# Decode in two stretches around the 256-column phase, P of three steps kept on chip, and a step's load put back

## The chip, the core and the metric

The kernel runs on one core of a Trainium2 chip. The metric is the device time of one execution in microseconds: the median over several runs. A profiled execution is used to read where the time goes; its times are counted in us from the first instruction (the span).

## The reference

Four batches of eight heads run a gated delta rule over 768 tokens with head size 48; the result goes through a mixture of four dense experts and then through a gated feed-forward block:

```python
for t in range(S):                              # attention, state is 48 x 48 per head
    y[:, :, t] = einsum('bhd,bhde->bhe', q[:, :, t], state)
    v_old = einsum('bhde,bhd->bhe', state, k_n[:, :, t])
    state = state + beta_t * outer(k_n[:, :, t], v[:, :, t] - v_old)
x = y as (3072 tokens, 384)
for e in range(4):                              # w1: 384 x 1024, w2: 1024 x 384
    out += p[:, e] * (relu(x @ w1[e]) @ w2[e])  # p: domain_probs, normalized
result = (sigmoid(out @ w_gate) * (out @ w_val)) @ w_out   # 384 x 1536 and back
```

All inputs are float32. The kernel gets the feed-forward block's weights as 64-bit words (`wp2`).

## The kernel before

**Products.** Every float32 product of the MoE is made of three matmuls in a rounded format: the weights are split into a high part (ScalarE, line 223) and a rest (VectorE, line 224), the tokens likewise. Weights come in granules of 128x768 floats (384 KB): `w_load` asks for one on SP's queue into one of three raw buffers, `w_split` splits it into one of four split buffers, `granule` does both some granules ahead of their use.

**Phases.** The 768 tokens of each sequence are cut into 12 steps of 64; a step has 256 columns of tokens, a pair of steps 512. A pair goes through the four experts ("m1") and then through the block ("m2"). Only the first pair is cut differently: expert 0 runs over step 0 alone, expert 1 over both steps, then comes expert 0 over step 1 alone, and so on. These two phases with 256 columns use up a granule in half the time. `EVENTS` lists the matmul groups of all phases in order.

**Attention steps.** Step c needs the matrices L and P (products of keys with keys and with queries, masked), the inverse X of a triangular matrix made from L (`inv_ops` on VectorE, two steps in one run, moved through DRAM to `XT` and `Ld`), and then a chain of small matmuls (`chain`): `ks_task`, `half_task` twice for the first runs, `tb_task`, `y_task`, `s_task`. The start-up makes L and P of steps 2 and 3 in the tiles `LP[0]` and `LP[1]`, masks them there, and those of steps 4 and 5 in DRAM (`raw_d`), from where `plan_g` fetches them into the same two tiles: step c uses `LP[c % 2]`, `Lts` and `Pts` are its two halves. `p_out` stores P of a step in DRAM (`pd`), `load_ys` reads it back into `YQ`, in two halves of 64 partitions, when the step's turn comes.

**Decode.** The 36 blocks ("parts") of the feed-forward block's weights arrive as 64-bit floats and are turned into 32-bit ones on the way: `dec_load` asks SP for 384 KB into one of five buffers, `dec_scale` is two operations on ScalarE (lines 264 and 265), `dec_join` three on VectorE, and `dec_store` puts 192 KB into `w2_d` from GpSimd's queue. The result of a part stands in one of four buffers up to part 7, in one of nine from part 8. All parts share memory with the inverse's tiles and later token tiles.

**Order.** Nothing is scheduled by the hardware: each engine runs its own list in order, and the lists are written by a planner at build time. `now` is the planned time, which grows by the matmuls of the MoE alone (a 512-column unit of an expert takes 3.885, a 256-column one 1.965; the phase over step 1 alone is planned from about 43 to 61). `plan(t, fn)` puts work at a planned time; `slot` emits what is due between matmul groups, `fill` emits the decode and the inverse from two lists, each in order. `pe_at` counts the matmuls emitted, attention included; `vec_at` is the planner's estimate of VectorE. Work marked "dve" is held while `vec_at` is more than `SLACK` = 2.8 ahead of `pe_at`. An emitted instruction still waits for its data; SP in particular issues each DMA only when its buffer is free, and what stands behind it on SP waits too.

Of the kernel before, what the change touches and what calls it, by code (L numbers as in the profile page):

```python
# [33 lines left out]
READ = 16.0  # L34
SERIAL = 0.12
FLIP, MOVE = 2, 4.0
INV2 = 0.0, 0.5, 78.0
AHEADD, LD, LS = 1.5, 6.0, 6.0
WARM = 11
WARM0, WARM1 = 2, 16  # L40
DEC0, DEC1, MORE = 17.0, 162.0, 8
CH1, CH2, TR1, TR2 = 66.0, 42.0, 42.0, 14.0

INV = [((0, 1), True), ((2, 3), True)]
# [25 lines left out]
NG1, NG2 = len(ORDER1) // 2, len(ORDER2) // 2  # L70
# [44 lines left out]
def moe_delta_kernel(  # L115
# [14 lines left out]
    nc = tc.nc  # L130


    pe_at, vec_at = [0.0], [0.0]
# [124 lines left out]
    def dec_load(n):  # L258
        dec_at[n] = pe_at[0]
        nc.sync.dma_start(out=dec_views(n)[0].bitcast(I32), in_=wp2[n].bitcast(I32))  # L260

    def dec_scale(n):
        r, low, high, t = dec_views(n)
        nc.scalar.activation(out=t, in_=high.bitcast(F32), func=AF.Copy, scale=2.0**-112)
        nc.scalar.activation(out=low, in_=low.bitcast(U32), func=AF.Copy, scale=2.0**-29)

    def dec_join(n):
        r, low, high, t = dec_views(n)
        ti = t.bitcast(I32)
        ts, stt, tt = vec.tensor_scalar, vec.scalar_tensor_tensor, vec.tensor_tensor  # L270
        return [
            lambda: ts(out=high, in0=high, scalar1=-(2**31), scalar2=None, op0=ALU.bitwise_and),
            lambda: stt(out=ti, in0=ti, scalar=3, in1=high, op0=ALU.logical_shift_left, op1=ALU.bitwise_or),
            lambda: tt(out=ti, in0=ti, in1=low, op=ALU.add),
        ]

    def dec_store(n):
        stored[0] = n + 1
        dec_at[n] = pe_at[0]
        nc.gpsimd.dma_start(out=w2_d[n // 2, :, (n % 2) * DM : (n % 2 + 1) * DM], in_=dec_views(n)[3])  # L280

    def plan_decode(t0, t1):
        def later(n, wait):
            return n < 0 or pe_at[0] > dec_at[n] + wait

        total = 2 * NG2
        gap = (t1 - t0) / total
        items = []
        for n in range(total):
            t = t0 + gap * n  # L290
            items.append((t - AHEADD * gap, "", lambda n=n: dec_load(n), lambda n=n: later(n - 5, LS)))
            items.append((t, "", lambda n=n: dec_scale(n), lambda n=n: later(n, LD)))
            for j, fn in enumerate(dec_join(n)):
                items.append((t + gap * (0.3 + 0.15 * j), "dve", fn))
            items.append((t + gap * 2.0, "", lambda n=n: dec_store(n)))
        items.sort(key=lambda r: r[0])
        back["dec"] += items


    x_hi, x_lo = {}, {}  # L300
# [20 lines left out]
    def load_ys(c):  # L321
        load_ki(c)
        if c == 1:
            return
        (q[1] or q[0]).dma_start(out=YQ[64:112, 0], in_=kq[c, 64:112, 1])
        (q[1] or q[0]).dma_start(out=YQ[0:C, 1], in_=kq[c, 0:C, 1])
        pd = pd_t.pop(c).rearrange("p (i h t) -> p i h t", i=2, h=H)
        q[0].dma_start(out=YQ[0:C, 0], in_=pd[0:C])
        q[0].dma_start(out=YQ[C:P, 1], in_=pd[C:P])
# [406 lines left out]
    def norm_late(c, i):  # L736
        t = tp.tile([P, 2 * STEP], F32, tag="tmp", name="kn2")[:, :DM]
        nc.sync.dma_start(out=t, in_=kt[c, :, i * DM : (i + 1) * DM])

        def rest():  # L740
            nc.scalar.square(out=t, in_=t)
            vec.tensor_reduce(
                out=w_all[:, 2 * c + i], in_=t.rearrange("p (h d) -> p h d", d=D), op=ALU.add, axis=mybir.AxisListType.X
            )

        return rest

    def plan_norms(c, t):
        for n in range(2):
            box = []  # L750
            plan(t + 13.0 * n, lambda c=c + n, box=box: box.extend(norm_late(c, i) for i in range(2)))
            plan(t + 13.0 * n + 7.0, lambda box=box: [fn() for fn in box])
        plan(t + 21.0, lambda: norms(c, c + 2))
        plan(t + 35.0, lambda: norm_move(c, c + 2))

    def norms(c0, c1):
        sl = slice(2 * c0, 2 * c1)
# [17 lines left out]
    def norm_move(c0, c1):  # L775
        sl = slice(2 * c0, 2 * c1)
        to, at = (t[:, sl].rearrange("p (c i) h -> p c i h", i=2) for t in (nrm_v, nrm_all))
        for i in range(2):
            for b in range(2):
                (q[1] or q[0]).dma_start(out=to[HALVES[i], :, b], in_=at[HALVES[b], :, i])  # L780
# [161 lines left out]
    def plan(t, fn, kind=""):  # L942
        todo.append((t, len(todo), kind, fn))
# [61 lines left out]
    def plan_chain(c, t, gap):  # L1005
        rows = chain(c)
        if c > 1:
            plan(t - (9.0 if c < 4 else 7.0 if c % 2 else 16.0), lambda: scale_v(c))
        if c > 1 and c % 2 == 0:

            def first():
                while inv_done[0] <= INV_OF[c][0]:
                    back["inv"].pop(0)[2]()
                if c > 2:
                    x_in(c)

            def one(n):
                q[2] = nc.sync
                put(*(x_parts(c) + off_parts(c))[n])

            plan(t - (30.0 if c == 2 else 13.0), first)
            for n in range(6 if c == 2 else 0):
                plan(t - 23.0 + 2.6 * n, lambda n=n: one(n))
        for r, row in enumerate(rows):
            plan(t + gap * r, lambda row=row: [fn() for fn in row], "pe")
        t1 = t + gap * len(rows)
        if c % 2 == 0 and c:
            plan(t1 - 2 * gap, lambda: (x_in(c + 1), off_in(c + 1)))
        if c >= FLIP:
            for n, fn in enumerate(x_move(c)):  # L1030
                plan(t1 - (2 if c < NC - 1 else 1) * gap + 4.0 + 1.4 * n, fn)
        if c + 1 < NC:
            plan(t + 2 * gap, lambda: (load_v(c + 1), load_ks(c + 1)))
            plan(t1 + 3.0 if c > 1 else 75.0, lambda: load_ys(c + 1))
        return t1
# [8 lines left out]
    def leave(c):  # L1044
        q[0] = nc.sync if c < 6 else nc.gpsimd
        l_out(c)
        p_out(c)
        q[0] = nc.gpsimd

    def plan_g(c, t):  # L1050
# [190 lines left out]
    with tc.manual_schedule():  # L1241
        pre_lo = xp.tile([P, KT, 2 * STEP], F32R, tag="xlo", name="pre_lo")
        dec_tiles()
        dpt = startup()
        q[1] = nc.sync
        vec_at[0] = 0.0
        plan(0.0, lambda: (gate_probs(dpt), load_p(0), load_p(1)))
        for i in range(2):
            plan(0.0, lambda i=i: s_task(0, i), "pe")
        plan(0.0, lambda: load_ys(1))  # L1250
        for c in (2, 3):
            back["dec"].append((4.0 + c, "dve", lambda c=c: (scale_p(c), p_out(c))))
        plan_chain(1, 1.0, 1.9)
        plan_tr(1, 12.0, 1.0)
        plan_inv(1, *INV2)
        plan_decode(DEC0, DEC1)
        for k in range(1, NPAIR):
            w = W[k]
            if k > 1:
                r0 = max(M2[0] + 44.0, w - 262.0)  # L1260
                plan_inv(k, r0, r0 + 17.0, w - CH1 - 20.0)
            if k + 1 < NPAIR:
                g0 = w - (161.0 if k > 1 else 116.0)
                plan_norms(2 * k + 2, g0 - 12.0)
                plan_g(2 * k + 2, g0)
                plan_g(2 * k + 3, g0 + 26.0)
            plan_chain(2 * k, w - (CH1 if k > 1 else 87.0), 5.9)
            plan_chain(2 * k + 1, w - (CH2 if k > 1 else 50.0), 5.9)
            plan_tr(2 * k, w - (TR1 if k > 1 else 26.0), 4.0)
            plan_tr(2 * k + 1, w - (TR2 if k > 1 else 9.0), 4.0)  # L1270
        todo.sort(key=lambda r: (r[0], r[1]))

        T, h = 0.0, {}
        for what, n, us in EVENTS:
            kind, b, e, s0, ns = PHASES[n]
            part = unit_us(kind, ns) / (2 if kind == "m1" else 3)
            if what == "b":
                now[0] = T = T + part * len(us)
                emit_b(n, us, [h.pop((n, u)) for u in us])
                slot()  # L1280
                continue
            if kind == "m1" and us[0] == 0:
                need = [(2 * b + s0 + s, i) for s in range(ns) for i in range(2)]
                while not all(q in x_done for q in need):
                    todo.pop(0)[3]()
            now[0] = T = T + part * (1 if kind == "m1" else 2)
            h[n, us[0]] = emit_a(n, us[0])
            slot()
            if us[0] == 3 and 0 < n < len(PHASES) - 1:
                load_p(n + 1)  # L1290
# [72 lines left out]
```

## Time and profile before

| | us |
|---|---|
| median of three runs | 1435.51 (1432.78 to 1441.81) |
| the profiled execution | 1437.48 |
| its span, first to last instruction | 1435.6 |
| TensorE busy (matmuls) | 1387.8 |
| VectorE busy | 1023.8 |
| ScalarE busy | 559.2 |

A windows row gives, for each stretch, its length and the busy time of PE, PEld, DVE, ACT and POOL in this order, with the count of instructions in brackets, then the granted clock of TensorE as a share of full speed, the busy share of the 16 DMA engines and what they moved. PE is TensorE's matmuls, PEld its weight loads, DVE VectorE, ACT ScalarE, POOL GpSimd, SP the engine that issues most DMAs. Tiles are shown without their numbers, so YQ stands for YQ and YQ1, and the buffers of the decode have the names of the tiles whose memory they use (dec_a, dec_b, Lpp).

### The profile page before, as it was taken

To read this page: it belongs to the slowest core of one execution; us is meant where nothing else is said; L and a number is where in the kernel's file an instruction comes from. 1 tells how busy PE (TensorE), PEld (TensorE's weight loads), DVE (VectorE), ACT (ScalarE), POOL (GpSimd) and SP (SyncE) were. 2 spreads that over 40 slices of the span, in tenths; PEclk is the share of its full clock that TensorE was granted. 3 is DMA by queue.
4 is the path that set the end of the run, shared out by engine and by line. 5 is a ranking of instruction groups with operands and counts; after the bars stand their busy time and mean duration, and the time that the engine had idled before them with its cause. 6 is when DMAs were issued, how large, how long until landed. Compare 5 with 4: busy or idle time off the path is not lost.

```text
span 1435.6 us, 25201 instructions
## 1 busy us (share of the span) xinstructions
PE 1387.8 (97%) x9939; PEld 1143.9 (80%) x9939; DVE 1023.8 (71%) x1809; ACT 559.2 (39%) x919; POOL 170.6 (12%) x235
## 2 busy tenths in 40 slices
PE   6889898999999999999999999999999999999998
PEld 5778776788878788888888788888888888888887
DVE  7658786866999677888667788767777755444553
ACT  3335453644323344332344432344333344333343
POOL 2310220310012210011300001310000210000000
PEclk6789999999999999999999999999999999999999
DMA  8876796995455874555765555775434662434331
GB/s 210 243 207 213 229 312 239 283 248 153 154 163 143 184 194 143 165 158 154 190 159 165 161 163 144 178 194 153 138 97 128 151 185 94 136 107 128 96 106 65
DMA packets 114790, 241.52 MB, mean 168 GB/s; under 512 B 38784, under 2 KB 43072, under 8 KB 113008
## 3 DMA queue, kind: packets, MB, share of 16 engines
q1 hardware_dynamic: 94368, 191.72, 44.2%
q0 software_dynamic: 15904, 46.23, 13.8%
q10 hardware_dynamic: 4400, 1.97, 0.6%
q8 instruction: 78, 1.28, 0.4%
q14 instruction: 40, 0.33, 0.1%
HBM read 197.38 MB, written 29.02 MB: 158 GB/s over the span
## 4 chain that ended last, share of the span: by engine, by line
PE 81%; DVE 7%; DMA 5%; issue 3%; SPq 1%; ACT 1%; POOL 1%; ACTq 0%; DVEq 0%; POOLq 0%
PE ph L834 43%; PE acc L871 33%; DVE Xpp L142 2%; DVE itmp L142 2%; DVE ws L142 1%; DMA raw<-in_wp 1%; PE pu L597 1%; DVE hlo L142 1%; PE ps L683 1%; PE pk L597 1%; PE pg L362 1%; PE yt L639 1%; DMA XT<-xd 1%; DMA dec_a<-in_wp 1%; PE yt L640 1%
## 5 line engine op out<-in xcount | busy, mean ns | idle before, releaser
L834 PE MATMUL ph<-xhi,ws 128*128 128x512 f32 (+1 forms) x2064 | 629.2, 388 | 8.2 <-DVE ws L142 6.9
L871 PE MATMUL acc<-hhi,ws 128*128 128x512 f32 (+1 forms) x1632 | 496.7, 386 | 8.1 <-DVE ctmp L142 3.0
L834 PEld LDWEIGHTS ph<-xhi,ws 128*128 128x128 f32 x2064 | 381.4, 188 | 87.1 <-DVE ws L142 7.7
L834 PE MATMUL ph<-xlo,ws 128*128 128x512 f32 (+1 forms) x1032 | 395.5, 386 | 0.6 <-DVE xlo L142 0.6
L871 PEld LDWEIGHTS acc<-hhi,ws 128*128 128x128 f32 x1632 | 304.0, 189 | 72.3 <-issue 6.0
L142 DVE TENSOR_TENSOR ws<-raw,ws 128x768 fp32r<-128x768 f32 x308 | 294.3, 961 | 40.0 <-ACT ws L223 36.7
L871 PE MATMUL acc<-hlo,ws 128*128 128x512 f32 (+1 forms) x816 | 314.3, 385 | 3.8 <-issue 1.9
L841 ACT ACTIVATE hhi<-ph 128x512 fp32r<-128x512 f32 (+1 forms) x200 | 116.2, 581 | 472.1 <-PE ph L834 465.1
L223 ACT CAST ws<-raw 128x768 fp32r<-128x768 f32 x308 | 251.9, 829 | 18.8 <-DMA raw<-in_wp 12.0
L142 DVE SCALAR_TENSOR_TENSOR hlo<-ph,hhi 128x512 fp32r<-128x512 f32 (+1 forms) x200 | 133.4, 667 | 148.1 <-ACT hhi L841 147.7
L834 PEld LDWEIGHTS ph<-xlo,ws 128*128 128x128 f32 x1032 | 194.2, 189 | 41.3 <-DVE xlo L142 2.5
L871 PEld LDWEIGHTS acc<-hlo,ws 128*128 128x128 f32 x816 | 154.3, 189 | 35.7 <-DVE hlo L142 3.2
L142 DVE TENSOR_TENSOR itmp<-Xpp,Lpp 128x62 f32<-128x62 f32 (+29 forms) x344 | 157.6, 465 | 6.5 <-DMA Lpp<-ls 1.1
L142 DVE TENSOR_TENSOR Xpp<-Xpp,itmp 128x62 f32<-128x62 f32 (+29 forms) x344 | 157.2, 464 | 5.8
L142 DVE TENSOR_TENSOR gv<-ph,sg 128x512 f32<-128x512 f32 x72 | 49.7, 691 | 95.6 <-PE ph L834 92.0
L850 ACT CAST hhi<-gv 128x512 fp32r<-128x512 f32 x72 | 44.7, 621 | 165.4 <-DVE gv L142 165.4
L142 DVE TENSOR_TENSOR hlo<-gv,hhi 128x512 fp32r<-128x512 f32 x72 | 50.2, 697 | 49.4 <-ACT hhi L850 49.4
L913 POOL DMA_DIRECT2D ACC<-ctmp x39 | 34.5, 1174 | 390.8 <-DVE ctmp L142 390.8
L848 ACT ACTIVATE sg<-ph 128x512 f32<-128x512 f32 x72 | 43.0, 597 | 42.8 <-PE ph L834 42.8
L442 POOL DMA_DIRECT2D ld<-LP x12 | 8.1, 675 | 322.9 <-DVE LP L142 231.5
L142 DVE TENSOR_TENSOR ctmp<-acc,pe 128x512 f32<-128x512 f32 (+1 forms) x57 | 35.4, 657 | 9.8 <-PE acc L871 9.1
L582 POOL TENSOR_TENSOR V<-V,nrm_v 128x384 f32<-128x384 f32 x22 | 22.1, 1044 | 37.8 <-DMA V<-in_vt 24.7
(171 smaller groups left out, 854.9 us busy)
## 6 DMA issues: line engine op xcount, KB each, us to landing
raw<-in_wp SPq DMA_DIRECT2D x200, 384.0 KB, 3.1
raw<-w_d SPq DMA_DIRECT2D x108, 384.0 KB, 3.5
ACC<-ctmp POOLq DMA_DIRECT2D x33, 256.0 KB, 5.6
KQ<-in_kg SPq DMA_DIRECT2D x7, 896.0 KB, 6.7
Lpp<-ld POOLq DMA_DIRECT2D x8, 768.0 KB, 9.1
pe<-p_d SPq DMA_DIRECT2D x23, 256.0 KB, 5.3
dec_a<-in_wp SPq DMA_DIRECT2D x15, 384.0 KB, 6.6
Lpp<-in_wp SPq DMA_DIRECT2D x14, 384.0 KB, 7.2
```

The costliest lines, as they stand in the source:

```text
L142: return fn(*args, **kw)
L223: nc.scalar.copy(out=w[:, 0], in_=t)
L362: nc.tensor.matmul(out=pg[i][b * C : (b + 1) * C, j], lhsT=src[b][ROWS[i], 0, h], rhs=src[b][ROWS[i], :, h], start=True, stop=True,)
L582: nc.gpsimd.tensor_tensor(out=V[:, b], in0=V[:, b], in1=nrm_v[:, 2 * c + b].unsqueeze(2).to_broadcast([P, H, D]), op=ALU.mult,)
L597: nc.tensor.matmul(out=ps[r][HALVES[k], h], lhsT=lhsT, rhs=rhs, start=True, stop=True)
L639: nc.tensor.matmul(out=dst[:, 0], lhsT=fa[:, cols], rhs=YQ[0:112, 0, i, h], start=True, stop=True)
L834: nc.tensor.matmul(out=res[q], lhsT=lt, rhs=rt, start=(k == 0 and j == 0), stop=(k == KT - 1 and j == 2))
L841: nc.scalar.activation(out=hh, in_=res[0], func=AF.Relu)
L848: nc.scalar.activation(out=sg, in_=res[0], func=AF.Sigmoid)
L850: nc.scalar.copy(out=hh, in_=gv)
L871: nc.tensor.matmul(out=acc_t[d][:, :w], lhsT=lt, rhs=rt, start=(u == 0 and j == 0), stop=(u == nf - 1 and j == 2),)
L913: nc.gpsimd.dma_start(out=a, in_=t, accum_op=ALU.add)
```

## The change

Decode: parts 0 to 12 are planned from 8 to 46, one per 2.92, no part from 46 to 66, and parts 13 to 35 from 66 to 157, one per 3.96; before, all 36 stood from 17 to 162, one per 4.03. A load may be asked for up to 13 ahead of the scale, though not until 1.5 after the planned time of the part behind the one that had its buffer; before it was 1.5 spacings ahead, 6.0. The buffer's gate counts 1.5 from the last join of the part five before (before: 6 from its store), the scale's gate 9 from the load (before: 6). The store stands 6.0 behind the scale, before 8.1.

P: steps 2, 3 and 4 no longer store P in DRAM and read it back; GpSimd copies it from `LP` to `YQ` in `load_ys`, two copies of 64x1024 per step. Since P of step 3 stays in `LP[1]` until then, the load of step 5 into that tile, the scaling of its L and its stores are planned 46 later. The six pieces of X and Ld of step 2 go from 18 ahead of the chain, one per 2.2, instead of 23 ahead, one per 2.6. The key loads for the norms start 4 and 3 earlier and get 11 instead of 7 before they are squared; the norms themselves come 1 later.

```diff
@@ -34,11 +34,12 @@
 READ = 16.0
 SERIAL = 0.12
 FLIP, MOVE = 2, 4.0
+HELD = 2, 3, 4
 INV2 = 0.0, 0.5, 78.0
-AHEADD, LD, LS = 1.5, 6.0, 6.0
+AHEADD, LD, LS = 13.0, 9.0, 1.5
 WARM = 11
 WARM0, WARM1 = 2, 16
-DEC0, DEC1, MORE = 17.0, 162.0, 8
+DEC, MORE = ((0, 8.0), (13, 46.0), (13, 66.0), (36, 157.0)), 8
 CH1, CH2, TR1, TR2 = 66.0, 42.0, 42.0, 14.0
 
 INV = [((0, 1), True), ((2, 3), True)]
@@ -274,27 +275,38 @@
             lambda: tt(out=ti, in0=ti, in1=low, op=ALU.add),
         ]
 
+    joined = {}
+
     def dec_store(n):
         stored[0] = n + 1
-        dec_at[n] = pe_at[0]
         nc.gpsimd.dma_start(out=w2_d[n // 2, :, (n % 2) * DM : (n % 2 + 1) * DM], in_=dec_views(n)[3])
 
-    def plan_decode(t0, t1):
-        def later(n, wait):
-            return n < 0 or pe_at[0] > dec_at[n] + wait
-
-        total = 2 * NG2
-        gap = (t1 - t0) / total
+    def plan_decode():
+        def later(at, n, wait):
+            return n < 0 or pe_at[0] > at.get(n, 1e9) + wait
+
+        def time(n):
+            for (n0, t0), (n1, t1) in zip(DEC, DEC[1:]):
+                if n < n1:
+                    return t0 + (t1 - t0) * (n - n0) / (n1 - n0), (t1 - t0) / (n1 - n0)
+
         items = []
-        for n in range(total):
-            t = t0 + gap * n
-            items.append((t - AHEADD * gap, "", lambda n=n: dec_load(n), lambda n=n: later(n - 5, LS)))
-            items.append((t, "", lambda n=n: dec_scale(n), lambda n=n: later(n, LD)))
-            for j, fn in enumerate(dec_join(n)):
-                items.append((t + gap * (0.3 + 0.15 * j), "dve", fn))
-            items.append((t + gap * 2.0, "", lambda n=n: dec_store(n)))
+        for n in range(2 * NG2):
+            t, gap = time(n)
+            t0 = max(t - AHEADD, sum(time(n - 5)) + LS if n >= 5 else 0.0)
+            items.append((t0, n, "", lambda n=n: dec_load(n), lambda n=n: later(joined, n - 5, LS)))
+            items.append((t, n, "", lambda n=n: dec_scale(n), lambda n=n: later(dec_at, n, LD)))
+            fns = dec_join(n)
+
+            def last(n=n, fn=fns[-1]):
+                fn()
+                joined[n] = pe_at[0]
+
+            for j, fn in enumerate(fns[:-1] + [last]):
+                items.append((t + gap * (0.3 + 0.15 * j), n, "dve", fn))
+            items.append((t + 6.0, n, "", lambda n=n: dec_store(n)))
         items.sort(key=lambda r: r[0])
-        back["dec"] += items
+        back["dec"] += [(r[0], *r[2:]) for r in items]
 
 
     x_hi, x_lo = {}, {}
@@ -324,6 +336,10 @@
             return
         (q[1] or q[0]).dma_start(out=YQ[64:112, 0], in_=kq[c, 64:112, 1])
         (q[1] or q[0]).dma_start(out=YQ[0:C, 1], in_=kq[c, 0:C, 1])
+        if c in HELD:
+            for b in range(2):
+                nc.gpsimd.tensor_copy(out=YQ[HALVES[b], b], in_=Pts[c % 2][HALVES[b]])
+            return
         pd = pd_t.pop(c).rearrange("p (i h t) -> p i h t", i=2, h=H)
         q[0].dma_start(out=YQ[0:C, 0], in_=pd[0:C])
         q[0].dma_start(out=YQ[C:P, 1], in_=pd[C:P])
@@ -748,10 +764,10 @@
     def plan_norms(c, t):
         for n in range(2):
             box = []
-            plan(t + 13.0 * n, lambda c=c + n, box=box: box.extend(norm_late(c, i) for i in range(2)))
-            plan(t + 13.0 * n + 7.0, lambda box=box: [fn() for fn in box])
-        plan(t + 21.0, lambda: norms(c, c + 2))
-        plan(t + 35.0, lambda: norm_move(c, c + 2))
+            plan(t + 14.0 * n, lambda c=c + n, box=box: box.extend(norm_late(c, i) for i in range(2)))
+            plan(t + 14.0 * n + 11.0, lambda box=box: [fn() for fn in box])
+        plan(t + 26.0, lambda: norms(c, c + 2))
+        plan(t + 40.0, lambda: norm_move(c, c + 2))
 
     def norms(c0, c1):
         sl = slice(2 * c0, 2 * c1)
@@ -1020,7 +1036,7 @@
 
             plan(t - (30.0 if c == 2 else 13.0), first)
             for n in range(6 if c == 2 else 0):
-                plan(t - 23.0 + 2.6 * n, lambda n=n: one(n))
+                plan(t - 18.0 + 2.2 * n, lambda n=n: one(n))
         for r, row in enumerate(rows):
             plan(t + gap * r, lambda row=row: [fn() for fn in row], "pe")
         t1 = t + gap * len(rows)
@@ -1044,7 +1060,8 @@
     def leave(c):
         q[0] = nc.sync if c < 6 else nc.gpsimd
         l_out(c)
-        p_out(c)
+        if c not in HELD:
+            p_out(c)
         q[0] = nc.gpsimd
 
     def plan_g(c, t):
@@ -1249,11 +1266,11 @@
             plan(0.0, lambda i=i: s_task(0, i), "pe")
         plan(0.0, lambda: load_ys(1))
         for c in (2, 3):
-            back["dec"].append((4.0 + c, "dve", lambda c=c: (scale_p(c), p_out(c))))
+            back["dec"].append((4.0 + c, "dve", lambda c=c: scale_p(c)))
         plan_chain(1, 1.0, 1.9)
         plan_tr(1, 12.0, 1.0)
         plan_inv(1, *INV2)
-        plan_decode(DEC0, DEC1)
+        plan_decode()
         for k in range(1, NPAIR):
             w = W[k]
             if k > 1:
@@ -1261,9 +1278,9 @@
                 plan_inv(k, r0, r0 + 17.0, w - CH1 - 20.0)
             if k + 1 < NPAIR:
                 g0 = w - (161.0 if k > 1 else 116.0)
-                plan_norms(2 * k + 2, g0 - 12.0)
+                plan_norms(2 * k + 2, g0 - 16.0)
                 plan_g(2 * k + 2, g0)
-                plan_g(2 * k + 3, g0 + 26.0)
+                plan_g(2 * k + 3, g0 + (26.0 if k > 1 else 72.0))
             plan_chain(2 * k, w - (CH1 if k > 1 else 87.0), 5.9)
             plan_chain(2 * k + 1, w - (CH2 if k > 1 else 50.0), 5.9)
             plan_tr(2 * k, w - (TR1 if k > 1 else 26.0), 4.0)
```

## Rows read from the trace of the kernel before

**Rows 1.** windows: us, busy us (instructions) per engine, clock, DMA share, GB/s

```profile
97.00:310.00 213.00, 197.56 (x1648) 163.75 (x1645) 164.34 (x316) 108.31 (x199) 42.70 (x66) 0.98 0.82 253
310.00:1430.00 1120.00, 1115.95 (x7040) 915.43 (x7039) 793.08 (x1281) 419.60 (x653) 100.80 (x131) 1.00 0.53 147
```

**Rows 2.** timeline of PE: start, us, line, operation, count, [idle before <- releaser]

```profile
161.42 1.02 PE L834 MATMUL ph<-xhi,ws 128*128 128x512 f32 x2 [3.74 <-DVE ws L142]
...
202.98 0.73 PE L834 MATMUL ph<-xhi,ws 128*128 128x512 f32 x2 [0.78 <-DVE ws L142]
...
207.74 0.47 PE L871 MATMUL acc<-hhi,ws 128*128 128x512 f32 x1 [2.42 <-DVE ctmp L142]
...
227.19 0.50 PE L871 MATMUL acc<-hhi,ws 128*128 128x512 f32 x1 [0.47 <-DVE ws L142]
...
233.92 0.70 PE L871 MATMUL acc<-hhi,ws 128*128 128x512 f32 x2 [1.68 <-DVE ws L142]
...
236.68 1.17 PE L871 MATMUL acc<-hhi,ws 128*128 128x512 f32 x2 [1.75 <-ACT hhi L841]
...
239.02 0.79 PE L871 MATMUL acc<-hlo,ws 128*128 128x512 f32 x1 [1.17 <-DVE hlo L142]
...
269.02 0.50 PE L834 MATMUL ph<-xhi,ws 128*128 128x512 f32 x1 [2.38 <-DVE ws L142]
```

**Rows 3.** windows at the two stretches of half clock, columns as above

```profile
161.70:165.10 3.40, 3.40 (x9) 2.62 (x9) 3.40 (x7) 1.59 (x3) 0.54 (x1) 0.50 0.57 160
236.80:243.60 6.80, 5.63 (x13) 3.94 (x14) 4.45 (x6) 0.62 (x1) 0.54 (x1) 0.50 0.47 170
```

**Rows 4.** chain of waits, 147 to 170 us: start, us, what

```profile
149.72 9.80 DMA raw<-in_wp
```

**Rows 5.** waits of ACT, 100 to 300 us: us in total, times, longest

```profile
ACT YQ L264 <- DMA dec_a<-in_wp: 13.2, 3, 7.2
...
ACT kn L741 <- DMA kn<-in_kt: 3.4, 1, 3.4
```

**Rows 6.** windows of line 264 alone, the first operation of each decoded part

```profile
97.00:138.00 41.00, 3.24 (x6) 1.00 0.65 212
138.00:166.00 28.00, 2.22 (x4) 0.94 0.67 201
166.00:225.00 59.00, 6.01 (x11) 1.00 1.01 300
225.00:305.00 80.00, 8.29 (x15) 0.96 0.81 260
```

**Rows 7.** timeline of DVE, the three operations that join a part

```profile
214.13 0.38 DVE L142 TENSOR_SCALAR Lpp<-Lpp 128x384 int32<-128x384 int32 x1
214.55 0.56 DVE L142 SCALAR_TENSOR_TENSOR YQ<-YQ,Lpp 128x384 int32<-128x384 int32 x1
215.25 0.56 DVE L142 CUSTOM_DVE_ANT_0 YQ<-Lpp,YQ 128x768 uint16<-128x768 uint16 x1
```

**Rows 8.** windows, all engines, ahead of the 256-column phase

```profile
97.00:138.00 41.00, 40.05 (x286) 34.30 (x283) 31.69 (x66) 22.23 (x41) 2.72 (x5) 1.00 0.65 212
```

**Rows 9.** timeline of POOL, 71 to 79 us

```profile
71.32 2.86 POOL L385 TENSOR_SCALAR_AFFINE_SELECT LP<-LP 64x1024 f32<-64x1024 f32 x2
```

**Rows 10.** timeline of DVE, 211 to 214 us, POOL multiplying V from 211.75

```profile
210.09 0.95 DVE L142 TENSOR_TENSOR ws<-raw,ws 128x768 fp32r<-128x768 f32 x1
...
212.02 1.59 DVE L142 TENSOR_TENSOR ws<-raw,ws 128x768 fp32r<-128x768 f32 x1
```

**Rows 11.** timeline of SP, first and last of step 5's five stores

```profile
253.47 0.42 SPq L442 DMA_DIRECT2D ld<-LP  x1
...
256.56 2.21 SPq L459 DMA_DIRECT2D pd<-LP  x1
```

**Rows 12.** DMA issues, 280 to 310 us: count, KB each, median us to landing

```profile
raw<-w_d SPq DMA_DIRECT2D x7, 384.0 KB, 10.0
```

**Rows 13.** waits of SP, 100 to 300 us

```profile
SPq L539 <- DMA xs<-Xpp: 4.7, 1, 4.7
```

## The prediction

> **What bounds the kernel now.** I read the busy time per stretch first. From 97 to 310 us TensorE works 197.6 of 213 us, and from 310 to 1430 us it works 1115.95 of 1120 [rows 1]. TensorE is the bound, and after 310 us only 4.05 us are left to win, in parts that the change hardly touches. So I look at the first 310 us alone. The start-up before 68 us is untouched by the diff.
>
> The timeline of TensorE then shows each place where it sat idle [rows 2]. I group them as the change would meet them. **A**: 3.74 us at 157.7. **B**: 0.78 and 2.42 us at 202 to 208. **C**: 0.47, 1.68, 1.75 and 1.17 us at 226.7 to 239. **D**: 2.38 us at 266.6. Together 14.4 of the 15.4 idle us. Right behind A and inside C the granted clock is 0.50 for 3.4 and 6.8 us, with TensorE busy for 3.40 and 5.63 us of them [rows 3]. Work at half clock loses half its time, so A carries 1.7 us more and C 2.8 us. A is worth 5.4, B 3.2, C 7.9 and D 2.4: **18.9 us** is all that the change can win.
>
> Who ends these waits? The planner's clock counts only the MoE's matmuls; the row at 161.42 is the first product behind the 256-column phase, planned at 60.6, so 97 us lie between the clocks ahead of A and 101 behind it; the product at 207.74 is planned at 99.4, 108 us apart. For A the chain of waits shows a weight load that took 9.80 us, issued at 149.72 as soon as VectorE had freed its buffer [rows 4]. For C the waits of ScalarE show the loads of the decode (D's load stands on SP behind five stores, below): 13.2 us in three waits on dec_a alone, the longest 7.2 [rows 5]. ScalarE runs in order, so the weight casts and the relu behind such a wait come late, and TensorE starves. The counts of decode scales per stretch show why: 6 parts are decoded by 138 us, 10 by 166, 21 by 225, and from 166 to 225 the DMA engines are busy 1.01 of their time at 300 GB/s [rows 6]. By the plan (17 + 4.03 n) 25 parts were due by 225 us, planned 116. A part's load waits for its buffer, the buffer for the store of the part five before, and that for late loads: the decode runs round its five buffers no faster than loads land.
>
> **The change, part by part.**
>
> *Decode earlier.* By the new plan 12 or 13 parts are decoded by 138 us instead of 6, none from 46 to 66 (about 140 to 166 us), then one per 3.96 against 4.03. A part costs VectorE 0.38 + 0.56 + 0.56 = 1.5 us [rows 7]. In the stretch from 97 to 138 VectorE is busy 31.69 of 41 us [rows 8]: six more parts make 31.7 + 9 = 40.7, just full. The planner holds vector work once it is 2.8 us behind, so at worst (nothing hidden) the overhang of some 2.5 us reaches TensorE; at best 0. I take 0.5, near the lower end, since the count still fits. DMA is busy 0.65 there [rows 6], so the 3.4 MB of six parts fit; the five loads asked for at once near planned 8 (2 MB, 7 us at the 300 GB/s of the full stretch) stand ahead of one or two weight loads. Bounds 0 to 3; I take 0.5.
>
> What it buys is A: four parts leave the phase (4 x 1.5 = 6 us of VectorE), buffers come free sooner, and the critical load starts some 2 to 3 us earlier. Bytes do not fall: loads 13 to 15 are due at 53, 57 and 61, inside the phase, 1.2 MB against the two loads and two stores there now. I let 4.4 of A's 5.4 go; bounds 0 and 5.4.
>
> *Loads longer ahead.* Up to 13 planned us before the scale, against 6.0; the scale may not be emitted until 9 us after the load, against 6; a buffer is asked for again 1.5 us after the join, not 6 us after the store. The longest wait was 7.2 us [rows 5], so 7 us more lead covers it nearly. Of C I let 6.2 of 7.9 go, of D 1.9 of 2.4. Bounds: half of both, or all. The added wait is on SP's queue: a load that stands there until VectorE has joined the part five before holds every weight load behind it (rivals).
>
> *P on chip.* Three stores of 512 KB (steps 2 to 4) and their loads back go, 3 MB; of these 1 MB lies in the full stretch. Added are six copies of 64x1024 on GpSimd; the nearest row is a pair of affine selects of that shape, 2.86 us [rows 9]. While GpSimd reads SBUF, VectorE slows: a 128x768 subtract took 1.59 us instead of 0.95 [rows 10]. So a pair costs VectorE between 0 and 2.9 us, three pairs 0 to 8.6, hidden behind granules that are subtracted some us before use. I take 0.5. SP's load of step 4 into the same tile, due at 78.6, now stands behind copies due at 75; 3.6 us cover 2.9. The copies wait, as the loads of P did, until the step before is done with YQ; decode stores queue behind them on GpSimd, whom only later granules need.
>
> *Step 5 postponed.* Its load of L and P (1 MB), its five stores (SP sits in them from 253.47 to 258.77 [rows 11], just ahead of the load that D waits for) move 46 planned us back. That helps C and D, counted above, and lands at 278 to 310 us, where weight loads already take 10.0 us [rows 12] although TensorE shows no wait there. The decode ends sooner there and step 3's P is not loaded, so bytes about balance. Cost between -0.5 and 4; I take 1.5, since all of it goes through SP, ahead of weights.
>
> *X of step 2 and the norms.* Pieces start 5 planned us later, so SP no longer stands 4.7 us for the store of X [rows 13]; norm loads get 11 instead of 7 us, against ScalarE's 3.4 us wait [rows 5]. Both waits lie just ahead of B. I let 1.7 of 3.2 go; bounds 0 and 3.2. SP issues as many pieces in the stretch as before, which is why not all.
>
> **Sum.** Gains 4.4 + 1.7 + 6.2 + 1.9 = 14.2; costs 0.5 + 0.5 + 0.5 + 1.5 = 3.0; net 11.2 us. The profiled execution took 1437.48 us (span 1435.6, 1.9 around it), so it becomes 1426.3. Its time is 2.0 above the median of the runs, 1435.51; the forecast for a median is **1424.3**.
>
> **Rivals.**
>
> *Nothing new binds* (chance 0.12): all 18.9 go, costs hide: 1435.5 - 18.9 = 1416.6. For it: every wait names a cause that the change moves. Against: the full DMA stretch.
> The Trainium skill speaks for it: its page "DMA: Bandwidth & Descriptors" (Specifications) gives about 358 GB/s as a core's limit to memory, so the 300 would leave a sixth free; by that the sum is this rival's 1416.6. Here the busy share of 1.01 at 300 GB/s [rows 6] speaks against that, and I let the row decide.
>
> *The DMA stays full* (0.22): from 166 to 225 the plan now wants 13 parts instead of 11, 1.2 MB more, which eats the 1 MB of P. Weight loads land as late as now; B stays whole (1.7 back), C keeps half (2.3 back), D 1.0 more: 1424.3 + 5.0 = about 1429.
>
> *It doesn't do what it says* (0.08): VectorE is full before planned 46, parts slip into the 256-column phase, ScalarE waits for one of only four result buffers (parts 4 to 7). A stays (4.4 back) and 2 us are added: about 1431.
>
> *SP is held* (0.06, the slower side): a load with only 1.5 us of grace stands on SP until VectorE's join, and weights behind it are late. A shows the price: a load later than its weights have spare stalls TensorE us for us. Taking 3 us as spare, about the 2.8 that the planner leaves VectorE, it decides from holds of 3 us on: if each of the 23 loads of the second stretch is held 4 us, 23 us pass through, 1424.3 + 23 = about 1447, and 1452 at 4.2 us. Against it: the load is planned 2.9 us behind that point, and the planner does not let VectorE fall further than 2.8.
>
> **How the numbers follow.** My own forecast has 0.52. Its bounds run from 1417 to 1432. The range from **1415 to 1434** holds it, the first three rivals, and leaves out the slower one. One per cent, 14.4 us, is about what a measurement of this kernel can tell from no change. Faster than 1421.2: the first rival and a third of my own, 0.30. Slower than 1449.9: 0.05. Within: 0.65.
>
> **What would show it.** Right: no half clock behind 161 and 237 us; no idle of 3 us on TensorE after 100; ScalarE's waits on dec_a from 13 us to below 3; 12 or 13 decode scales by 138 us, at most two from there to the end of the phase. Wrong: TensorE waiting for ws near 200 to 225 with DMA at 1.0 (second rival); new waits at 280 to 320; SP waiting on VectorE at line 260's load (the last rival). What would upset the sum most is a wait that TensorE's gaps hide now because a longer one ends later.

## The result, and the profile after

The changed kernel takes **1419.56 us** (median of four runs, 1419.13 to 1422.24); the kernel before took 1435.83 on the same chip. The ratio is 0.9886, interval 0.9851 to 0.992: 16.3 us less, where 11.2 were forecast. The profiled execution took 1419.64 us, its span is 1417.9. In the changed kernel's file line 834 is 850, 871 is 887, 597 is 613, 264 is 266, 260 is 261, 215 is 216, 142 is 143, 223 is 224. In two of the experiments, e1 and e6, the profiled execution ran at a mean granted clock of 0.84 and 0.56 and took 1543.76 and 2291.1 us: it is left out of their times, and its rows are not read.

The busy time per stretch of the changed kernel, columns as in [rows 1] (the second stretch ends with this span):

```profile
97.00:310.00 213.00, 207.19 (x1738) 173.11 (x1737) 173.11 (x322) 114.22 (x208) 47.21 (x67) 0.99 0.80 247
310.00:1412.00 1102.00, 1100.12 (x6917) 902.84 (x6916) 785.64 (x1273) 413.05 (x640) 100.17 (x129) 1.00 0.52 147
```

TensorE's idle time from 97 to 310 us fell from 15.4 to 5.8 us, at a clock of 0.99 for 0.98. All that TensorE waits for between 100 and 300 us is in four rows (columns: waiter, what it waited for, us in total, times, longest):

```profile
PE ph L850 <- DVE xlo L143: 2.7, 1, 2.7
PE acc L887 <- DVE ctmp L143: 2.0, 1, 2.0
PE ph L850 <- ACT xhi L720: 0.6, 1, 0.6
PE pu L613 <- DVE R L143: 0.4, 2, 0.3
```

No row names ws any more, which five of the eight places of [rows 2] did. A, C and D are gone. The two large rows are these places in the timeline of TensorE:

```profile
109.46 0.80 PE L850 MATMUL ph<-xlo,ws 128*128 128x512 f32 x1 [2.66 <-DVE xlo L143]
...
201.90 0.70 PE L887 MATMUL acc<-hhi,ws 128*128 128x512 f32 x2 [2.03 <-DVE ctmp L143]
```

The second is what is left of B. The first is new. Windows behind the two:

```profile
108.90:112.30 3.40, 2.84 (x7) 2.26 (x8) 2.24 (x4) 0.00 (x0) 0.54 (x1) 0.50 0.94 326
201.90:209.70 7.80, 7.80 (x34) 6.46 (x35) 7.59 (x12) 2.47 (x5) 6.50 (x8) 1.00 1.09 225
```

So the half clocks of [rows 3] went, and one of 3.4 us came, behind the new wait. The decode's scales per stretch, columns as in [rows 6]:

```profile
97.00:138.00 41.00, 6.07 (x11) 0.96 0.65 217
138.00:166.00 28.00, 1.67 (x3) 1.00 0.78 240
166.00:225.00 59.00, 6.54 (x12) 1.00 1.03 322
225.00:305.00 80.00, 5.45 (x10) 1.00 0.73 215
```

11 parts by 138 us (6 before), 26 by 225 (21 before), while the DMA engines stay full from 166 to 225, at 322 for 300 GB/s. ScalarE no longer waits for any part's load: the 13.2 us of [rows 5] are 0, and of ScalarE's waits for loads this one is the longest:

```profile
ACT ws L224 <- DMA raw<-in_wp: 9.9, 7, 2.9
```

The wait moved to SP, which now stands in front of the decode's loads (line 261) until VectorE has freed their buffers; the six largest of these rows:

```profile
SPq L261 <- DVE Xpp L143: 15.7, 6, 6.0
...
SPq L261 <- DVE dec_a L143: 6.4, 1, 6.4
...
SPq L261 <- DVE YQ L143: 4.0, 4, 1.3
SPq L261 <- DVE dec_b L143: 3.7, 2, 2.8
SPq L261 <- DVE Lpp L143: 3.7, 2, 3.2
SPq L261 <- DVE itmp L143: 3.4, 2, 1.8
```

That is 36.9 us in 17 waits, with weight loads queued behind them, and TensorE waits for none of them.

### The profile page after: what moved, and what is told of

It is laid out like the page before. It is cut to its first block, busy times and chain, and to the rows that moved or that the text cites. A ratio compares the mean times of both kernels' runs of the same rounds, so it can differ in the third digit from the quotient of the medians.

```text
span 1417.9 us, 25215 instructions
## 1 busy us (share of the span) xinstructions
PE 1380.9 (97%) x9939; PEld 1140.5 (80%) x9939; DVE 1026.0 (72%) x1809; ACT 559.4 (39%) x919; POOL 172.8 (12%) x233
## 4 chain that ended last, share of the span: by engine, by line
PE 79%; DVE 11%; DMA 5%; issue 2%; ACT 1%; SPq 1%; ACTq 0%; POOL 0%; DVEq 0%
PE ph L850 42%; PE acc L887 32%; DVE Xpp L143 2%; DVE ws L143 2%; DVE itmp L143 2%; DMA raw<-in_wp 2%; DVE hlo L143 1%; PE pu L613 1%; PE ps L699 1%; PE pk L613 1%; PE pg L378 1%; PE yt L655 1%; DMA Lpp<-ls 1%; PE yt L656 1%; ACT ws L224 1%
```

## The experiments

**The measure by place.** The same matmul (counted, not timed) opens each section in every trace, so a section's length can be compared between kernels. The table is worked out from the starts of these matmuls; sections are named by the time of before, numbers are us against before (first line: its own lengths). Two traces of one kernel (the change and e13) differ by up to 1.4 us in a section, and by 2.8 in B, so smaller differences are not read alone.

```
                         to 111  111-144  A 144-165  B 165-210  C 210-247  D 247-288  288-493  to end    span
before                   111.23    32.80      21.14      44.72      36.88      41.32   205.20  942.31  1435.60
the change                +1.24    +0.04      -5.76      -1.34      -8.61      -1.47    -1.60   -0.18   -17.68
e13 the change again      +1.68    +1.47      -5.94      +1.45      -8.61      -1.58    -0.56   -0.15   -12.24
e2  no new decode         -0.74     0.00      -1.84      -0.77      -7.80      -2.46    -2.04   +0.39   -15.26
e11 only new decode       +3.57    +1.41      -5.68      +2.85      -7.99      -2.00    +1.90   -0.50    -6.43
e7  P through DRAM        +5.05    +1.05      -6.08      +2.19      -7.68      -2.27    +2.18   -0.10    -5.66
e8  old X and norms       +1.82    +1.10      -5.73      +0.81      -8.59      -1.37    -1.62   -1.03   -14.61
e3  no pause              +1.53    +0.66      -5.12      -1.19      -8.61      -2.45    -0.98   +1.36   -14.76
e4  short lead            +0.70     0.00      -5.44      +0.41      -8.59      -2.26    -0.96   -0.71   -16.86
e5  start at 14           +0.38     0.00      -6.12      +0.59      -8.58      -1.57    -0.42   +0.54   -15.16
e10 old times             +0.37     0.00      -5.01      -2.38      -8.61      -2.43    -2.29   -0.12   -20.46
e12 two pauses            +1.10    +0.02      -6.00      -2.42      -8.61      -1.05    -2.60   -0.28   -19.83
```

e1 and e6 have no line; e11 is e1's kernel once more, for its rows. In e2's file line 834 is 839.

**The first theory and its rival.** From the change's trace: the new decode plan takes A and C, the postponed step 5 takes D, and the rest is small. The rival: the time comes from the bytes that no longer move (P's three round trips, and step 5's out of the full stretch).

**e1_decode_only, e11_decode_only_look** put everything back but the decode's plan, lead and gates:

```diff
-HELD = 2, 3, 4
+HELD = ()                                    # P of 2 to 4 through DRAM again
...
-plan_g(2 * k + 3, g0 + (26.0 if k > 1 else 72.0))
+plan_g(2 * k + 3, g0 + 26.0)                 # step 5 as before; X pieces and norms too
...
```

> The new decode plan alone (start, pause, loads ahead, gates); P, step 5, X pieces and norms as before. Theory 1 (the decode plan removes the waits at the 256-column phase and most of those at 226 to 239 us, the rest is small): about 1426, the first of the two waits gone, some 2 us of idle left near 267. Rival (the bytes of P and of step 5 made the loads late, the plan does little): 1433 to 1437 with the 3.7 us wait behind the phase or the waits on dec_a still there.

> The new decode plan alone again, for a profile at full clock. Theory 2: 1427 to 1431, the waits at 226 to 239 us mostly gone, but 2 us or more at 190 to 208 (P's loads) and 1 to 2.4 us near 260 behind step 5's five stores on SP. Rival (the plan alone also removes the wait near 260): no wait of 1 us between 210 and 300.

Measured: e1 1428.47, ratio 0.9958 (0.9942 to 0.9974); e11 in its one run 1430.88. That lies between the theory and its rival in e1; e11's rows have 4.0 us of idle at B, ended by VectorE and not by one of P's loads, and no wait of 1 us between 210 and 300, as the rival said.

**e2_p_step5_only** is the other half, made from the kernel before: P of 2 to 4 kept on chip and step 5 postponed, decode, X and norms as they were.

> P of steps 2 to 4 kept on chip and step 5's load and stores put back 46; decode, X pieces and norms as before. Theory 1: 1429 to 1432, the 3.7 us wait and the half clock behind the 256-column phase still there, the wait near 267 gone. Rival (bytes): 1422 to 1426, with both big waits gone.

Measured: 1422.88, ratio 0.9928 (0.9904 to 0.9953): some 10 us, against 6 for the decode's plan. The rival's time was met, but not its sign, since the wait at A stays. By place the halves do not add. TensorE in the stretch of C in the kernel before, then in e2, then in e11 (there with the stretch of D behind it), columns as in [rows 1]:

```profile
222.00:245.00 23.00, 17.93 (x124) 13.24 (x123) 13.88 (x24) 8.77 (x17) 2.17 (x4) 0.85 0.77 285
```
```profile
222.00:245.00 23.00, 22.52 (x319) 17.99 (x319) 20.41 (x36) 12.17 (x22) 2.16 (x4) 1.00 0.60 205
```
```profile
222.00:245.00 23.00, 22.98 (x271) 18.55 (x270) 18.00 (x31) 12.04 (x22) 1.71 (x4) 1.00 0.68 243
262.00:275.00 13.00, 13.00 (x116) 10.37 (x115) 8.29 (x16) 9.13 (x17) 2.04 (x4) 1.00 0.84 264
```

Idle 5.1 us before, 0.5 in e2, none in e11: either half alone takes away C, and D too (the table: -2.46 and -2.00). A is different. e2 keeps its idle time, though not its half clock:

```profile
160.41 0.73 PE L839 MATMUL ph<-xhi,ws 128*128 128x512 f32 x2 [3.47 <-DVE ws L143]
```

**e3_no_pause, e4_short_lead, e5_late_start** take one part of the new decode plan back each:

```diff
-DEC, MORE = ((0, 8.0), (13, 46.0), (13, 66.0), (36, 157.0)), 8
+DEC, MORE = ((0, 8.0), (36, 157.0)), 8                            # e3
+DEC, MORE = ((0, 14.0), (13, 46.0), (13, 66.0), (36, 157.0)), 8   # e5
...
-AHEADD, LD, LS = 13.0, 9.0, 1.5
+AHEADD, LD, LS = 6.0, 6.0, 1.5                                    # e4
```

> The changed kernel with one stretch from 8 to 157, no pause. Theory 1: the wait behind the 256-column phase comes back with its half clock, 4 to 5 us: about 1424. Rival (only the earlier start and the lead count): 1419 to 1420, no such wait.

> The changed kernel with loads only 6 ahead and the scale's gate at 6, as before. Theory 1: ScalarE waits on dec loads again, 5 us or more in sum between 170 and 260 us, and 3 to 5 us of time come back: 1422 to 1425. Rival (the lead isn't what counted, since loads land sooner now): 1419 to 1420, ScalarE's waits on dec loads under 2 us.

> The changed kernel with the first 13 parts from 14 to 46 instead of 8 to 46. Theory 1 (the new 2.66 us wait at 106.8 us and the half clock behind it come from decode joins on VectorE ahead of step 1's xlo): the wait falls back to about 0.4, no half clock near 109, 3 to 4 us less: about 1416. Rival (VectorE is then too full at one part per 2.46, and the loss moves behind 110 us): 1419 to 1421 with new waits between 110 and 160.

Measured: 1421.11 (0.9901, 0.9874 to 0.9927), 1420.69 (0.9899, 0.9873 to 0.9925) and 1421.64 (0.9904, 0.9881 to 0.9927). None can be told from the change, and A is gone in all three. In e4 ScalarE waits 3.7 us for the decode's loads, between what the theory and its rival said. In e5 the wait near 107 us falls to 1.4 us, not 0.4, without a half clock behind it, and the total is no shorter. The pause is not what removes A; the windows of the phase (138 to 161 us) in the kernel before, the change and e3 say why it cannot be:

```profile
138.00:161.00 23.00, 19.59 (x144) 18.29 (x142) 16.52 (x37) 10.19 (x21) 4.36 (x6) 1.00 0.69 207
```
```profile
138.00:161.00 23.00, 22.89 (x161) 21.24 (x160) 19.87 (x44) 11.65 (x22) 4.36 (x6) 1.00 0.77 234
```
```profile
138.00:161.00 23.00, 22.51 (x158) 20.88 (x157) 20.26 (x46) 13.05 (x26) 4.88 (x7) 1.00 0.87 254
```

VectorE (third busy time) is busier in the phase than before, not freer (TensorE also does more there), and in e3 four parts are scaled inside it:

```profile
138.00:161.00 23.00, 2.18 (x4) 1.00 0.87 254
```

**e6_step5_back, e7_p_dram, e8_x_norms_back** each undo one of the other parts.

```diff
-plan_g(2 * k + 3, g0 + (26.0 if k > 1 else 72.0))
+plan_g(2 * k + 3, g0 + 26.0)                 # e6
-HELD = 2, 3, 4
+HELD = 2, 4                                  # e6: P of step 3 through DRAM too
+HELD = ()                                    # e7
...
-plan(t - 18.0 + 2.2 * n, lambda n=n: one(n))
+plan(t - 23.0 + 2.6 * n, lambda n=n: one(n)) # e8, with the norms' old times
...
```

> The changed kernel with step 5's load and stores where they were, so P of step 3 goes through DRAM; P of 2 and 4 stays on chip. Theory 1 (its five stores on SP held up the load that ScalarE waited for near 264): 1421 to 1423, with new waits between 215 and 260. Rival (the longer lead covers it): 1419 to 1420.

> The changed kernel with P of steps 2 to 4 through DRAM again, step 5 still postponed. Theory 1: 3 MB more in DMA, 0 to 2 us: 1419 to 1421. Rival (bytes are the bound from 166 to 225): 1423 to 1426, with weight loads late at 190 to 225.

> The changed kernel with the X pieces of step 2 and the norms of all pairs at their old places. Theory 1: SP stands for X's store and ScalarE for the key loads again, 1 to 3 us between 180 and 205: 1420 to 1422. Rival (the decode plan covers it): 1419 to 1420.

Measured: e6 1419.96 (0.9897, 0.9876 to 0.9918), level with the change: postponing step 5 and keeping P of step 3 on chip, which e6 undoes together, show no price or gain beyond the width of the interval, some 6 us. e8 1424.24 (0.9924, 0.9906 to 0.9943), inconclusive: its interval overlaps that of the change and its sections are within 1.1 us of those of e13. **e7** 1427.39 (0.9946, 0.9926 to 0.9967): P's round trips cost some 4 to 9 us (by the ratios 0.9946 against 0.9886 and e13's 0.9889, of 1436: 8 to 9; by the medians against 1419.56 and e13's 1423.45: 7.8 and 3.9), and the time is longer than either theory said. By place they cost up to 111 us and between 288 and 493; in B e7 is longer than the change by 3.5 us, but than e13 by 0.7 only. Two of TensorE's waits in e7, of which the first was 3.37 us in e13 too:

```profile
209.26 0.70 PE L887 MATMUL acc<-hhi,ws 128*128 128x512 f32 x2 [3.69 <-DVE ctmp L143]
```
```profile
482.95 1.38 PE L613 MATMUL pu<-R,XT 64*64 64x48 f32 x62 [2.40 <-DMA XT<-xd]
```

**The second theory.** It was that the early start of the decode (planned 8) is what frees the phase, and that a kernel with the old times would get A back. The rival: the new gates and the lead do it, and the early start costs, because its joins stand ahead of step 1's tokens on VectorE.

**e10_old_times** keeps all of the change but the two stretches; **e12_two_pauses** starts at 16, pauses also from 90 to 101, and scales L of step 4 later; **e13_after_again** is the change itself, timed on the same chip in turn with them.

```diff
-DEC, MORE = ((0, 8.0), (13, 46.0), (13, 66.0), (36, 157.0)), 8
+DEC, MORE = ((0, 17.0), (36, 162.0)), 8                                                   # e10
+DEC, MORE = ((0, 16.0), (13, 46.0), (13, 66.0), (19, 90.0), (19, 101.0), (36, 157.0)), 8  # e12
-plan(t + 14, lambda: scale_l(c))
+late = 12.0 if c == 4 else 0.0
+plan(t + 14 + late, lambda: scale_l(c))                                                   # e12; leave(c) too
```

> The changed kernel with the decode's old times (all 36 parts from 17 to 162), the new gates and the load up to 13 ahead kept, P and step 5 as in the change. Theory 2 (the start at 8 is what freed the 256-column phase; P and step 5 freed the rest): the wait behind the phase comes back in part, 3 to 4 us and its half clock, and nothing near 107 us: 1421 to 1424. Rival (the gates and the lead did it): no wait behind the phase, and without the loss near 107 it is 1415 to 1418.

> The changed kernel with the first part at 16, a second pause from 90 to 101, and step 4's scaling of L and its stores 12 later. Theory 2 (both waits that are left, 2.7 us at 106.8 and 2.0 us at 199.9 with a half clock behind either, are decode and scaling work on VectorE ahead of what TensorE waits for): both under 1 us, no half clock behind 100: 3 to 6 us less than the changed kernel in the same call. Rival (VectorE's work only moves): within 1 us of it, new waits between 110 and 250.

> The changed kernel itself, beside the others of this call: 1418 to 1422.

Measured: e10 **1417.67** (1417.25 to 1417.89), ratio 0.9855 (0.9833 to 0.9877); e12 1418.02 (1414.98 to 1419.32), 0.9855 (0.983 to 0.988); e13 1423.45 (1420.83 to 1425.07), 0.9889 (0.9861 to 0.9918). The intervals of the ratios touch, but all four runs of e10 and of e12 lie below all four of e13. e13 came out above its range. The second theory fell for A: e10 has none (-5.01). What it said of the two waits that are left held: in e12 they are 0.39 and 1.02 us, no half clock follows, and e12 is 5.4 us below e13. The busy time per stretch of e10:

```profile
97.00:310.00 213.00, 210.34 (x1791) 176.39 (x1792) 173.20 (x327) 117.57 (x214) 47.20 (x67) 1.00 0.83 257
...
97.00:138.00 41.00, 40.04 (x291) 34.30 (x292) 31.87 (x67) 22.78 (x43) 2.73 (x5) 1.00 0.64 202
```

TensorE is idle for 2.7 us, where it was 5.8 in the change, and the clock is 1.00. Both of the change's larger waits are shorter in e10, and both are a matter of VectorE's order. The timeline of VectorE in the change, from the first tokens of step 1 to the second:

```profile
104.94 0.55 DVE L143 TENSOR_TENSOR xlo<-pt,xhi 128x384 fp32r<-128x384 f32 x1
105.41 0.55 DVE L143 CUSTOM_DVE_ANT_0 Xpp<-dec_a,Xpp 128x768 uint16<-128x768 uint16 x1
105.87 1.08 DVE L143 TENSOR_TENSOR ACC<-acc,pe 128x256 f32<-128x256 f32 x3
...
107.11 0.35 DVE L143 TENSOR_SCALAR dec_b<-dec_b 128x384 int32<-128x384 int32 x1
...
107.65 0.55 DVE L143 SCALAR_TENSOR_TENSOR dec_b<-dec_b 128x384 int32<-128x384 int32 x1
108.12 0.35 DVE L143 TENSOR_TENSOR Xpp<-Xpp,itmp 128x192 f32<-128x192 f32 x1
108.39 0.55 DVE L143 CUSTOM_DVE_ANT_0 dec_b<-dec_b 128x768 uint16<-128x768 uint16 x1
108.86 0.55 DVE L143 TENSOR_TENSOR xlo<-pt,xhi 128x384 fp32r<-128x384 f32 x1
```

And in e10, where nothing of the decode stands there and VectorE itself waits for TensorE:

```profile
107.90 0.42 DVE L143 TENSOR_TENSOR ACC<-acc,pe 128x256 f32<-128x256 f32 x1 [0.66 <-PE acc L887]
108.24 0.33 DVE L143 TENSOR_TENSOR Xpp<-Xpp,itmp 128x175 f32<-128x175 f32 x1
108.61 0.36 DVE L143 TENSOR_TENSOR itmp<-Xpp,Lpp 128x192 f32<-128x192 f32 x1
109.00 0.36 DVE L143 TENSOR_TENSOR Xpp<-Xpp,itmp 128x192 f32<-128x192 f32 x1
109.28 0.55 DVE L143 TENSOR_TENSOR xlo<-pt,xhi 128x384 fp32r<-128x384 f32 x1
```

TensorE waits 0.39 us here in e10 and 2.66 in the change. At B the change's VectorE does two steps of a join between hlo and ctmp:

```profile
199.61 0.68 DVE L143 SCALAR_TENSOR_TENSOR hlo<-ph,hhi 128x512 fp32r<-128x512 f32 x1
200.21 0.35 DVE L143 TENSOR_SCALAR dec_a<-dec_a 128x384 int32<-128x384 int32 x1
200.59 0.56 DVE L143 SCALAR_TENSOR_TENSOR YQ<-YQ,dec_a 128x384 int32<-128x384 int32 x1
201.07 1.88 DVE L143 TENSOR_TENSOR ctmp<-acc,pe 128x512 f32<-128x512 f32 x3
```

e10's ctmp begins at 199.89, right behind hlo (199.28), and TensorE's wait is 1.10 us instead of 2.03: the two steps take 0.91 by their rows, the difference is 0.93. (What is left in e10 is ended by ScalarE's hhi.)

## Why the prediction was right or wrong

The total was right in direction and size: 1419.56 against 1424.3, within 1415 to 1434. Its terms were not all right, and that it came out so near is in part luck: the gain of P on chip, taken as nothing, and the price of the early start, taken too low, pull opposite ways.

**What bounds the kernel** held: everything before 68 us and after 310 is nearly as it was, except 0.6 to 1.6 us between 288 and 493 that were not foreseen. In the change 1.33 of them are one wait for XT (0.38 us at 472, where it was 1.71 at 488 before); in e13 it is 1.43, so this part is not steady.

**A** was sized at 4.4 and gave 5.8: all of it. The reason given ("four parts leave the phase", so VectorE is freer) is wrong: VectorE is busier there, e3 scales four parts in it, and A is gone. Neither the lead (e4) nor the early start (e10) is needed, each taken by itself; no run with the new gate lacks both. What every kernel without A shares, and e2 lacks, is the gate that lets a buffer be asked for 1.5 us after its join instead of 6 us after its store (and the store due 6.0 us behind the scale instead of 8.1, twice the old 4.03).

The weight load of [rows 4], which TensorE waited for, is the next one that SP issues behind the load of pe. SP's list around it, before and in the change:

```profile
148.10 0.43 SPq L812 DMA_DIRECT2D pe<-p_d  x1
148.58 0.45 SPq L260 DMA_DIRECT2D Lpp<-in_wp  x1
149.72 4.39 SPq L215 DMA_DIRECT2D raw<-in_wp  x3
```
```profile
148.21 0.45 SPq L828 DMA_DIRECT2D pe<-p_d  x1
149.36 0.33 SPq L216 DMA_DIRECT2D raw<-in_wp  x1
149.74 0.66 SPq L261 DMA_DIRECT2D Lpp<-in_wp  x1
```

This load starts 0.36 us earlier in the change, not 2 to 3, but it lands after 7.0 us instead of 9.8. In e2, which keeps A, it takes 9.5 us, in e10 6.2, and in all ten traces without A 5.9 to 7.3. Before and in e2 a load of the decode (Lpp, 384 KB) goes out right ahead of it on SP and is still under way; in none of the ten is a load of the decode under way when this one is issued. So the wait came and went with the order on SP's queue, not with VectorE's room. By the 300 GB/s of [rows 6] the 384 KB are about 1.3 us, an estimate, of the 2.8; where the rest comes from stays open. Whether the gate alone changes the order on the kernel before was not run: that is argued, not shown.

**C and D** were sized at 6.2 and 1.9 and gave 8.6 and 1.5. The longer lead was named as their cause, and that was not shown. Either half of the change takes both away: e2, with the old lead, loses C (-7.80) although ScalarE there still waits 6.9 us for dec_a, and e11, with P in DRAM, loses it by the decode's plan (-7.99). Which part of that plan does it was not taken apart: e4, with the lead at 6, loses C too (-8.59), but has P on chip. The prediction counted each stall once, under the lead, with a word on step 5, and so the sum could come out; the step that failed is the cause: P on chip with step 5 postponed takes both away without the lead.

**B** was sized at 1.7 and is the least steady place: -1.34 in the change, +1.45 in e13, the same kernel. The idle time there was 2.03 us in the first, 3.37 in the second, with half clock behind it only in the second. X and the norms had been named for it; e8 could not show that. What shows is VectorE's order (e10).

**The denser first stretch** was costed at 0.5 + 0.5 and is mis-sized. The working asked if VectorE would be full (40.7 of 41 us). It was not: 35.06 us busy with 11 parts. But the end of one join and all of the next, 2.0 us, stood between the two halves of step 1's tokens in VectorE's order, and TensorE waited 2.27 us longer and then worked 2.84 us at half clock, which is 1.4 more: 3.7 at this place. TensorE had come there 2.35 us earlier than before (the product behind the wait starts at 109.46, before at 109.54), so up to 111 us the net against before is only +1.24, in e13 +1.68 and 1.47 more by 144; with the later starts of e10, e5 and e12 it is +0.37, +0.38 and +1.10 and nothing more by 144. That is 0.2 to 2.8 us, in part near the spread.

**P on chip** was the term that the prediction missed most. It gave the 3 MB no gain of their own and charged 0.5 for the copies. By e7 it is worth some 4 to 9 us, and the decode's plan alone gives 6 of the 16 (e1). How the transfers cost that much was not taken apart: the longer of e7's two waits shown is on VectorE (3.69), not on a load, and nearly as long in e13.

**Step 5 postponed** was costed at 1.5 and no price shows: 288 to 493 us is shorter than before, and e6 is level.

**The rivals.** "The DMA stays full" was right about the DMA (1.03, 322 GB/s) and wrong about the consequence: TensorE waits for no weight there. "SP is held" shows its sign, 36.9 us of SP standing at line 261, and no price: single holds of 6.0 and 6.4 us, twice the 3 us taken as spare, made no weight late for TensorE. "Nothing new binds" (1416.6) is what e10 nearly is, once the two stretches are left out. "It doesn't do what it says" is true in one sense not foreseen: the two stretches, for which the change is named, bring nothing that the rest of the change does not bring without them (e10).

**What would show it.** Right: no half clock behind 161 and 237; no idle of 3 us (2.66 at most, though 3.37 in e13); ScalarE's waits on dec_a from 13.2 to 0. Nearly right: 11 scales by 138 us for 12 or 13, and three from there to 166 for at most two. The last rival's sign, SP waiting on VectorE for the decode's loads, came as well.

## What to carry to other kernels

When several edits are aimed at the same stall, price the stall once and undo the edits one by one afterwards: C and D went with either half of this change, and the part thought cheap and incidental (P kept on chip) carried about as much as the whole new plan of the decode. When work is moved into a stretch with room, busy time is not enough of a test; read the order of the queue at the place where the bound engine's next operand is made. Here 2.0 us of joins ahead of one 0.55 us subtract cost TensorE a wait longer by 2.3 us and a stretch of half clock, on a VectorE that was idle for 6 of 41 us; and one decode load ahead of a weight load on SP came with the 3.7 us at A. A version with old times and new gates (e10) is the one to keep: 1417.67, ratio 0.9855, with e12 level.

## What the runs showed of the hardware that was not expected

How long TensorE idles does not by itself tell whether a half clock follows. In e13 3.37 us of idle at B were followed by 7.5 us at a mean of 0.79; windows of e13 and, behind 3.47 us of idle at A, of e2:

```profile
204.90:212.40 7.50, 7.48 (x26) 6.08 (x27) 7.26 (x11) 1.61 (x4) 6.49 (x8) 0.79 1.11 227
```
```profile
160.00:170.00 10.00, 9.60 (x50) 8.27 (x51) 10.00 (x22) 6.85 (x13) 1.75 (x4) 1.00 0.72 242
```

The kernel before had 3.74 us at A and then the half clock [rows 2, 3], but 2.42 us at B [rows 2] and none (1.00 from 166 to 225 [rows 6]). In e7 a shorter idle, 2.40 us at 480.55, was followed by one:

```profile
483.70:491.00 7.30, 7.30 (x49) 5.92 (x42) 4.49 (x7) 1.36 (x2) 1.67 (x2) 0.77 1.01 212
```

So an idle time of 2 to 4 us may cost itself alone or 1.4 to 1.7 us more (2.84 us at half clock in the change; 7.3 and 7.5 us at 0.77 and 0.79), and the same kernel got one and the other at B, behind 2.03 and 3.37 us. That may be part of why the runs of the change spread from 1419.13 to 1425.07; it is not shown, since e12, with no idle time above 1.02 us at these places, spread over 4.3 us too.
